# Second layer of a convolution and hard-swish kernel: P4's copies behind P2's C2, S2's chunks in another order, S4's negations behind the seed

## The chip, the cores and the metric

The kernel runs on one core of one Trainium2 chip. The metric is the device time of one execution in microseconds (us). Five engines of the core work side by side, each through its own instructions in order: TensorE (PE in the profile, its weight loads PEld), VectorE (DVE), ScalarE (ACT), GpSimd (POOL) and SyncE (SP). GpSimd and SyncE also issue transfers (DMAs). Semaphores order the engines among each other; they are put in by the framework from the order in which the program issues its instructions.

## The reference

```python
def _attn_ref(x, weight):                 # x (8, 4096, 192), weight (8, 7)
    w = np.exp(weight - np.max(weight, axis=-1, keepdims=True))
    w = w / (np.sum(w, axis=-1, keepdims=True) + 1e-09)
    x_pad = np.concatenate([np.zeros((B, K - 1, D)), x], axis=1)
    x_unf = x_pad[:, idx, :].reshape(B, S, K, H, group)
    return np.einsum('hk,bskhg->bshg', w, x_unf).reshape(B, S, D)

def _moe_ref(x, w_in, w_out):             # x (32768, 192), w_in (192, 2048), w_out (2048, 192)
    h = x @ w_in
    g = h * np.clip(h + 3.0, 0.0, 6.0) / 6.0
    return (g @ w_out).astype(np.float32)
```

A causal convolution of seven taps, one set of taps for each head, is followed by two matrix products with a hard-swish between them.

## The kernel before

The 32768 tokens are cut into 32 blocks of 1024. Block 0 is done in a plain way; blocks 1 to 31 each run `first_layer` and then `second_layer`. The first layer (matmuls of line 511) forms h from three parts of y (HIGH, LOW, MIX) and writes the gated g. The second layer (matmuls of line 653) forms g times w_out, and the change lies there.

**The fast product.** g is one tile of 8 chunks with four quarters each: A11, A21, A12, A22. w_out has B11, B12, B21, B22. The product is taken by a scheme of seven products in place of eight, with sums of the quarters as operands: S1 (kept in A21's place), S2 = S1 - A11 (kept in A11's place), S3 (a tile of its own, called `s` in the profile) and S4 = A12 - S2, which replaces S3 in its tile. Product 1 is A11 B11, 2 is A12 B21, 3 is S4 B22, 4 uses A22, 5 uses S1, 6 uses S2, 7 uses S3. Their results are called P1 to P7. Parts of products 1, 2, 4 and 5 are taken once more by the same scheme, at half size; those small products are written n.m here, so 2.7 is the seventh small product of product 2. Their operand sums lie in `shared` (of product 1), `sums2` (tile `z`, of 2), `sums4` (of 4) and `s5` (of 5, kept in A22's place).

**Accumulators.** PSUM is one tile of 8 banks, 128 rows by 512 columns each. In the second layer the banks are called x_, b, y_, c, a, f and h. Rows go by quadrants of 32: `first`, `second`, `third`, `fourth`; `lo` and `hi` are the halves of the columns, `m` the first 96 rows. The chains of the small products lie in x_ and y_: chain 2 (of P4) in rows 64 to 95 and chain 3 (of P1, later P5) in rows 96 to 127, each with A and E in the two halves of x_, and B and C in those of y_. A2, E2, B2, C2 and D2, the places of P2's small products, lie in f and h. A chain is continued by copies of ScalarE: B starts from a copy of A, C from a copy of B.

**The schedule.** The order is written out by hand. Four streams of matmuls, one for each strip of 32 output rows (strips 0 to 3), are put on a clock of 80 units; a matmul with 512 columns costs 2 units and runs as two passes, one with 256 columns costs 1. All other work is put among them by `do(t, ...)`, and everything is issued in order of these times, with t counted from half a unit earlier:

```python
def do(t, fn, *args, **kw):
    streams[3].append((t - 0.5, lambda: fn(*args, **kw)))
...
events = sorted(((t, fn) for st in streams for t, fn in st), key=lambda x: x[0])
```

So a number in `do` is a place in the order, for ScalarE, VectorE, GpSimd and SyncE each, not a time.

**What the steps below speak of**, by line:

- `level_two` (lines 740 to 754): the small products of P4 (strip 2, units 0 to 36), P1 (strip 3, units 0 to 36) and P5 (strip 3, units 44 to 76), each followed by its copy. Copies of step 1 are line 743 (B from A, here called B3 for P5), 2 line 744, 6 line 745 (C from B), 5 line 746, 7 line 747, 3 line 748. P4 is gathered in `shared`, P1 in `z`.
- Lines 815 and 816: two copies of b's first quadrant into P4's third. They must come before the seed, which overwrites that quadrant.
- Line 819: C2 from B2, wanted by small product 2.7 on strip 0 at unit 36. Line 820: D2 from B2, wanted at unit 60. Line 822: a copy inside bank a, wanted by strip 3 at unit 40; line 824 another, wanted at unit 60.
- The fill: product 5's matmuls on strip 3 that write the fourth quadrant of bank b, at units 4, 36, 48 and 76 (lines 760 and 761). "The fill" below is that of units 36 to 40.
- Line 841: S2 by pairs of chunks 02, 13, 46, 57 (line 458 in the profile, `g<-g`). S1, which it reads, comes from transfers that add two neighbouring chunks at a time. Product 6 reads S2 from unit 44 on.
- `fold` (lines 709 to 711): two sums of VectorE on P1 or P4; the second reads the chain's B in bank y_.
- Lines 844, 845 and 849: the small sums of S1 (line 603 in the profile, `g<-g`), wanted by P5's small products from unit 52 on.
- Line 847, the seed: P1 is copied to the first 96 rows of bank b (line 650, `psum<-z`), on which product 6 adds from unit 44.
- Line 851, the negations: S4 is made by ScalarE (line 572, `s<-g`: S3's tile becomes minus S2) and by a transfer that GpSimd issues (line 569) and that adds A12. Product 3 reads it from unit 64, in chunk order 0, 2, 1, 3, 4, 6, 5, 7.
- `between` (line 1125): split_high (ScalarE, line 476, at 48.4) and split_low (VectorE, line 1080, at 57) make parts of the next block's y.
- Lines 852 and 853: P7 is copied from bank c, and U3 is the sum of bank b and P7 (VectorE, line 458), to be read before product 3 adds to b at unit 64.

Of the kernel before, what the change touches and what calls it, by code (L numbers as in the profile page):

```python
# [25 lines left out]
def kernel(  # L26
# [8 lines left out]
    nc = tc.nc  # L35
# [10 lines left out]
    D2 = P // 2  # L46
# [41 lines left out]
    for base, dma in ((0, nc.scalar), (D2, nc.sync)):  # L88
        dma.dma_start(
            out=w_sb[base : base + D2],  # L90
            in_=weight.unsqueeze(1).to_broadcast([H, GJ, KC]),
# [126 lines left out]
    for n in range(AHEAD):  # L218
# [8 lines left out]
        out=e_sb[:], in0=w_sb[:], in1=mx[:].to_broadcast([P, KC]), op=ALU.subtract  # L227
# [47 lines left out]
    S2, S1, S4 = A11, A21, A12  # L275
# [5 lines left out]
    def take():  # L281
        return free_banks.pop(0)
# [163 lines left out]
    def rows(q):  # L446
        return slice(q * QS, (q + 1) * QS)
# [9 lines left out]
    def add(out, x, y, op=ALU.add):  # L457
        nc.vector.tensor_tensor(out=out, in0=x, in1=y, op=op)  # L458
# [126 lines left out]
    chunk_pairs = [slice(n, n + 3, 2) for n in (0, 1, 4, 5)]  # L585
# [35 lines left out]
    def second_layer(i, between):  # L621
        last = i + 1 == NB
        ours = [free_slots.pop(0) for _ in range(3)]
        x_, b, y_, c, a, _ = (psum[:, 2 * n + k] for n in ours for k in range(2))
# [3 lines left out]
        s5 = A22  # L628
        copy = nc.scalar.copy
        m = slice(0, DH)  # L630
        lo, hi = halves
        both = nc.sync, nc.scalar
        first, second, third, fourth = (rows(q) for q in range(4))
# [5 lines left out]
        A2, E2, C2, B2, D2 = f[first, lo], f[second, hi], h[first, lo], h[second, hi], h[third, hi]  # L639
# [3 lines left out]
        clock = [0] * 4  # L643
# [5 lines left out]
        def do(t, fn, *args, **kw):  # L649
            streams[3].append((t - 0.5, lambda: fn(*args, **kw)))  # L650
# [23 lines left out]
        def small(n, m_, out, start=False, j=3):  # L674

            x, w = prod[n]
            sums, ws = {
                1: (shared, w_s[:, 0]), 5: (s5, w_s[:, 1]), 2: (sums2, w_s[:, 2]),
                4: (sums4[0], w_s[:, 3]),
            }[n]  # L680
            x11, x12, x21, x22 = four_parts(x)
            z1, z2, z3, z4 = four_parts(sums)
            b11, t3, b21, b22 = quarters(w)
            t1, t2, t4 = (ws[:, k] for k in range(3))
            xm, wm = {
                1: (x11, b11), 2: (x12, b21), 3: (z4, b22), 4: (x22, t4),
                5: (z1, t1), 6: (z2, t2), 7: (z3, t3),
            }[m_]
            for u in range(NP // 2):
                put(j, 1, lambda u=u: matmul(  # L690
                    j, out, wm[:, u], xm[:, u], start and u == 0
                ))
# [45 lines left out]
        p4 = Fourth()  # L738

        def level_two(n, p, order, j=3):  # L740
            A, E, B, C = chains[j]
            steps = {
                1: lambda: copy(out=B, in_=A),
                2: lambda: copy(out=p()[first, lo], in_=A),  # L744
                6: lambda: copy(out=C, in_=B),
                5: lambda: copy(out=p()[second, lo], in_=E),
                7: lambda: copy(out=p()[second, hi], in_=C),
                3: lambda: copy(out=p()[first, hi], in_=C),
            }
            to = {1: A, 2: A, 6: B, 5: E, 7: C, 3: B, 4: C}  # L750
            for k in order:
                small(n, k, to[k], k in (1, 5), j)
                if k != 4:
                    do(clock[j] + (8.1 if k == 2 and n != 5 else 0.02 if n == 4 else 0), steps[k])

        rest = 6, 2, 7, 5, 4, 3
        chunks, first_fill = list(every), [True]
# [31 lines left out]
        p3(1)  # L789

        level_two(4, lambda: p4, (1,), 2)
        plain(2, c, 7, 2, every[:4], True)
        level_two(4, lambda: p4, rest, 2)
        plain(2, c, 7, 2, every[4:])
        plain(2, b, 6, 2, every)
        small(2, 3, D2, False, 2)
        p3(2)

        level_two(1, lambda: p1, (1,))
        fill_half(0, 2) if last else fill(2)  # L800
        plain(3, a, 2, 2, every[2:5] if last else every[2:4], True)
# [11 lines left out]
        assert clock == [80] * 4  # L813

        for t in halves:
            do(30 if t == hi else 29, copy, out=p4[third, t], in_=b[first, t])
        do(25.5, copy, out=p1[third], in_=b[second])
        do(20, copy, out=B2, in_=A2)
        do(31.9, copy, out=C2, in_=B2)
        do(45, copy, out=D2, in_=B2)  # L820
        do(12, copy, out=a[second], in_=a[fourth])
        do(34, copy, out=a[fourth], in_=a[second])
        do(40, lambda: copy(out=p2(second, hi), in_=C2))
# [13 lines left out]
        do(7, small_sums, sums2, A12, (3, 2), nc.vector)  # L837
        do(7, small_sums, sums4[0], A22, (4,), nc.vector)
        do(7, small_sums, sums2, A12, (1,), nc.vector)
        for r, when in zip(chunk_pairs, (28.5, 32.5, 28.6, 36.1)):  # L840
            do(when, lambda r=r: add(S2[:, r], S1[:, r], A11[:, r], ALU.subtract))
        do(32, tiles)
        do(36.03, fold_with, p1)
# [2 lines left out]
        do(36.05, fold_with, p4, 2)  # L846
        do(40 if last else 38.7, copy, out=b[m], in_=p1)
        do(21, last_sum, sums2, A12)
        do(36.3, small_sums, s5, S1, (1, 4), nc.vector)
        for r, t in zip(chunk_pairs, (30.5, 36.3, 42.1, 44.2)):  # L850
            do(t, negative, r)
        do(56.5, lambda: copy(out=late["p7"], in_=c[m]))
        do(60.2, lambda: add(late["u3"], b[m], late["p7"]))
# [83 lines left out]
    with tc.manual_schedule():  # L937
# [4 lines left out]
            out=c_sb[:], in0=e_sb[:], in1=sm[:].to_broadcast([P, KC]), op=ALU.mult  # L942
# [14 lines left out]
        b = take()  # L957
        for _ in range(3):

            nc.tensor.matmul(  # L960
                out=psum[:, b], lhsT=zeros[:, 0:P], rhs=zeros[:], start=True, stop=True
# [58 lines left out]
        n = 3  # L1020
        for slot, (c, group) in enumerate(parts):
            first = slot < len(early)
# [92 lines left out]
        for i in range(1, NB):  # L1115
            jobs = {n: [tap] for n, tap in zip((-1, 1, 3, 5, 7), taps)}
            jobs[-1] = left + jobs.get(-1, [])
            first_layer(i, jobs)
            def begin_conv():
                x_tiles[i + 2] = load_x(i + 2)  # L1120
                conv[:] = conv_jobs(i + 2)

            between, conv = [], []
            if i + 1 < NB:
                between += [(48.4, split_high), (57, split_low), (70, split_mix)]
                between += [
                    (t, lambda n=n: swap_parts(nc.gpsimd, (n,)))
                    for n, t in ((HIGH, 69), (LOW, 69), (MIX, 71))
                ]
            if i + 2 < NB:  # L1130
                between += [(1, begin_conv), (61.5, lambda: conv[0]()), (62, lambda: conv[1]())]
            left = second_layer(i, between)
            taps = conv[2:]
# [33 lines left out]
```

## Time and profile before

| | |
|---|---|
| median of 3 runs | 2220.82 us (2220.43 to 2220.97) |
| the profiled execution | 2220.51 us |
| its span in the profile | 2218.7 us |
| TensorE busy | 2201.0 us, 99% |
| VectorE busy | 1985.3 us, 89% |
| ScalarE busy | 1741.4 us, 78% |
| GpSimd busy | 1182.7 us, 53% |
| granted TensorE clock | 0.999 |

A block from the second on takes 68.07 us: about 35 in the second layer (80 units, of 0.43 us each) and 33 in the first. How to read the profile: times are us from the start of the span; a row names the engine, the line of the kernel, the operation, and the tiles as written and read. Matmuls are pipelined and their ends are modelled, so a stop of TensorE is read best from where its matmuls start. Idle time before an instruction is put down to the releaser that came last. The block shown below starts its second layer at 1017.95.

### The profile page before, as it was taken

To read this page: it belongs to the slowest core of one execution; us is meant where nothing else is said; L and a number is where in the kernel's file an instruction comes from. 1 tells how busy PE (TensorE), PEld (TensorE's weight loads), DVE (VectorE), ACT (ScalarE), POOL (GpSimd) and SP (SyncE) were. 2 spreads that over 40 slices of the span, in tenths; PEclk is the share of its full clock that TensorE was granted. 3 is DMA by queue.
4 is the path that set the end of the run, shared out by engine and by line. 5 is a ranking of instruction groups with operands and counts; after the bars stand their busy time and mean duration, and the time that the engine had idled before them with its cause. 6 is when DMAs were issued, how large, how long until landed. Compare 5 with 4: busy or idle time off the path is not lost.

```text
span 2218.7 us, 55332 instructions
## 1 busy us (share of the span) xinstructions
PE 2201.0 (99%) x22984; PEld 1481.5 (67%) x22984; DVE 1985.3 (89%) x1983; ACT 1741.4 (78%) x2391; POOL 1182.7 (53%) x1033
## 2 busy tenths in 40 slices
PE   9999999999999999999999999999999999999998
PEld 5467666667766676666677666766667666667765
DVE  8898998889898989988999988989898998889877
ACT  7488787787877878877878778787788787787876
POOL 2456544565544666445655446564456544565544
PEclk9999999999999999999999999999999999999999
DMA  6277778777778777787777888777877778777777
GB/s 157 60 137 146 141 145 151 141 145 141 145 138 159 136 141 143 146 156 133 146 142 145 144 151 143 141 139 144 160 131 145 139 147 153 138 146 140 132 141 117
DMA packets 353308, 313.20 MB, mean 141 GB/s; under 512 B 212480, under 2 KB 265216, under 8 KB 353056
## 3 DMA queue, kind: packets, MB, share of 16 engines
q0 software_dynamic: 114976, 234.46, 58.9%
q1 hardware_dynamic: 236840, 74.93, 16.7%
q8 instruction: 180, 2.95, 0.5%
q14 instruction: 72, 0.59, 0.1%
q10 hardware_dynamic: 1240, 0.27, 0.1%
HBM read 31.72 MB, written 25.17 MB: 26 GB/s over the span
## 4 chain that ended last, share of the span: by engine, by line
PE 93%; ACT 4%; issue 1%; DVE 0%; DMA 0%; SPq 0%; DVEq 0%; ACTq 0%
PE psum L511 46%; PE psum L653 44%; PE psum L296 2%; PE psum L341 2%; ACT s L572 1%; ACT shared L650 1%; ACT z L744 1%; ACT shared L744 1%; ACT psum L650 1%; DMA x<-in_x_dram 0%; DVE shared L458 0%; DVE g L603 0%; SPq L100 0%; DVE shared L464 0%; DVE g L458 0%
## 5 line engine op out<-in xcount | busy, mean ns | idle before, releaser
L653 PE MATMUL psum<-g,w_out 128*32 128x512 f32 (+1 forms) x5968 | 825.7, 503 | 0.0
L306 DVE SCALAR_TENSOR_TENSOR g<-g,psum 128x1024 f32<-128x1024 f32 (+1 forms) x528 | 618.8, 1185 | 107.3 <-ACT g L302 106.9
L653 PE MATMUL psum<-s,w_out 128*32 128x512 f32 (+1 forms) x3024 | 713.7, 586 | 0.0
L302 ACT ACTIVATE g<-psum,half 128x1024 f32<-128x1024 f32 (+1 forms) x528 | 565.4, 1088 | 5.7 <-PE psum L511 4.9
L511 PE MATMUL psum<-y_own,w_in 64*128 64x512 f32 x4464 | 523.3, 389 | 0.0
L511 PE MATMUL psum<-y_other,w_in 64*128 64x512 f32 x4464 | 516.0, 386 | 0.0
L523 ACT ACTIVATE psum<-psum 128x1024 f32<-128x1024 f32 x465 | 468.7, 1008 | 48.7 <-PE psum L511 46.6
L653 PEld LDWEIGHTS psum<-g,w_out 128*32 128x32 f32 x5968 | 338.5, 110 | 245.5 <-issue 111.4
L511 PEld LDWEIGHTS psum<-y_own,w_in 64*128 64x128 f32 x4464 | 413.5, 184 | 117.7 <-issue 26.0
L511 PEld LDWEIGHTS psum<-y_other,w_in 64*128 64x128 f32 x4464 | 418.1, 184 | 87.8
L603 POOL TENSOR_TENSOR shared<-g,shared 128x256 f32<-128x256 f32 x248 | 357.6, 1442 | 88.4 <-DVE g L306 57.0
L1057 DVE SCALAR_TENSOR_TENSOR y<-x,c_sb,y 128x1536 f32<-128x1536 f32 x186 | 335.2, 1802 | 1.5 <-ACT y L1055 1.3
L653 PE MATMUL psum<-g,w_s 128*32 128x256 f32 x1488 | 283.3, 379 | 0.3 <-DVE g L603 0.3
L569 POOL DMA_DIRECT2D s<-g x124 | 148.4, 1197 | 214.1 <-PE psum L653 124.2
L653 PE MATMUL psum<-z,w_out 128*32 128x256 f32 x992 | 235.1, 380 | 9.0 <-ACT psum L650 9.0
L569 POOL DMA_DIRECT2D g<-g x124 | 181.8, 1530 | 103.9 <-DVE s L414 103.9
L653 PE MATMUL psum<-z,w_s 128*32 128x256 f32 x992 | 227.5, 379 | 0.0
L653 PEld LDWEIGHTS psum<-s,w_out 128*32 128x32 f32 x3024 | 192.8, 110 | 51.2 <-issue 14.0
L266 POOL DMA_DIRECT2D y_other<-y_own x90 | 48.1, 534 | 280.2 <-issue 280.2
L458 DVE TENSOR_TENSOR g<-g 128x1024 f32<-128x1024 f32 x124 | 149.0, 1222 | 43.6 <-PE psum L653 30.9
L603 POOL TENSOR_TENSOR shared<-g 128x256 f32<-128x256 f32 x124 | 91.9, 741 | 170.3 <-DVE g L306 170.3
L650 ACT COPY psum<-psum 32x512 f32<-32x512 f32 x186 | 82.9, 446 | 116.4 <-PE psum L653 113.3
(115 smaller groups left out, 2955.9 us busy)
## 6 DMA issues: line engine op xcount, KB each, us to landing
y_other<-y_own POOLq DMA_DIRECT2D x180, 384.0 KB, 7.8
g<-g POOLq DMA_DIRECT2D x124, 512.0 KB, 6.1
s<-g POOLq DMA_DIRECT2D x124, 512.0 KB, 6.4
z<-g POOLq DMA_DIRECT2D x62, 512.0 KB, 7.5
out_dram<-shared SPq DMA_DIRECT2D x378, 64.0 KB, 4.2
x<-in_x_dram SPq DMA_DIRECT2D x53, 388.5 KB, 5.7
z<-g SPq DMA_DIRECT2D x31, 512.0 KB, 3.3
stage<-in_moe_w_in_dram SPq DMA_DIRECT2D x16, 192.0 KB, 4.4
```

The source lines that it names most:

```text
L266: dma.dma_start(out=to[D2:P], in_=part[0:D2])
L296: nc.tensor.matmul(out=psum[:, b], lhsT=w[r], rhs=src, start=start, stop=stop, skip_group_check=onto,)
L302: nc.scalar.activation(r6, h, ACT.Relu, bias=half[:], scale=1.0 / 6.0)
L306: nc.vector.scalar_tensor_tensor(out=g_, in0=g_, scalar=1.0, in1=h, op0=ALU.min, op1=ALU.mult)
L458: nc.vector.tensor_tensor(out=out, in0=x, in1=y, op=op)
L511: nc.tensor.matmul(out=psum[:, 2 * slots[n] + k], lhsT=r32(w_in_parts[part][r, c, s]), rhs=r32(y_other[0][r, part, s] if group else y_own[ ...
L523: nc.scalar.mul(both(n), both(n), 4097.0)
L569: nc.gpsimd.dma_start(out=out, in_=x, accum_op=ALU.add)
L603: engine.tensor_tensor(out=o, in0=p, in1=q, op=op)
L650: streams[3].append((t - 0.5, lambda: fn(*args, **kw)))
L653: nc.tensor.matmul(out=out, lhsT=w, rhs=x, start=start, stop=True, tile_position=(0, j * QS), skip_group_check=True,)
L1057: jobs.append(lambda k=k: nc.vector.scalar_tensor_tensor(out=y[:], in0=x[:, :, k : k + N], scalar=c_sb[:, k : k + 1], in1=y[:], op0=ALU.mu ...
```

## The change

Only places in the order change; no instruction is added or removed. P4's step 2 copy moves from 28.1 to 39.3, the two copies of line 816 from 29 and 30 to 35 and 35.1, D2's copy from 45 to 39.6. S2 was taken by chunks 02, 46, 13, 57 and is taken by 02, 13, 46, 57, the last of them now behind the small sums 3 and 2 of S1. The second and fourth negations move from 36.3 to 39.7 and from 44.2 to 48.3.

```diff
@@ -751,7 +751,8 @@
             for k in order:
                 small(n, k, to[k], k in (1, 5), j)
                 if k != 4:
-                    do(clock[j] + (8.1 if k == 2 and n != 5 else 0.02 if n == 4 else 0), steps[k])
+                    late_by = {(1, 2): 8.1, (4, 2): 19.3}.get((n, k), 0.02 if n == 4 else 0)
+                    do(clock[j] + late_by, steps[k])
 
         rest = 6, 2, 7, 5, 4, 3
         chunks, first_fill = list(every), [True]
@@ -813,11 +814,11 @@
         assert clock == [80] * 4
 
         for t in halves:
-            do(30 if t == hi else 29, copy, out=p4[third, t], in_=b[first, t])
+            do(35.1 if t == hi else 35, copy, out=p4[third, t], in_=b[first, t])
         do(25.5, copy, out=p1[third], in_=b[second])
         do(20, copy, out=B2, in_=A2)
         do(31.9, copy, out=C2, in_=B2)
-        do(45, copy, out=D2, in_=B2)
+        do(39.6, copy, out=D2, in_=B2)
         do(12, copy, out=a[second], in_=a[fourth])
         do(34, copy, out=a[fourth], in_=a[second])
         do(40, lambda: copy(out=p2(second, hi), in_=C2))
@@ -837,7 +838,7 @@
         do(7, small_sums, sums2, A12, (3, 2), nc.vector)
         do(7, small_sums, sums4[0], A22, (4,), nc.vector)
         do(7, small_sums, sums2, A12, (1,), nc.vector)
-        for r, when in zip(chunk_pairs, (28.5, 32.5, 28.6, 36.1)):
+        for r, when in zip(chunk_pairs, (28.5, 32.5, 32.6, 36.3)):
             do(when, lambda r=r: add(S2[:, r], S1[:, r], A11[:, r], ALU.subtract))
         do(32, tiles)
         do(36.03, fold_with, p1)
@@ -846,8 +847,8 @@
         do(36.05, fold_with, p4, 2)
         do(40 if last else 38.7, copy, out=b[m], in_=p1)
         do(21, last_sum, sums2, A12)
-        do(36.3, small_sums, s5, S1, (1, 4), nc.vector)
-        for r, t in zip(chunk_pairs, (30.5, 36.3, 42.1, 44.2)):
+        do(36.4, small_sums, s5, S1, (1, 4), nc.vector)
+        for r, t in zip(chunk_pairs, (30.5, 39.7, 42.1, 48.3)):
             do(t, negative, r)
         do(56.5, lambda: copy(out=late["p7"], in_=c[m]))
         do(60.2, lambda: add(late["u3"], b[m], late["p7"]))
```

On ScalarE the order from unit 28 to 48.4 was: P1's and P4's step 5, P4's step 2, P1's step 2, the two copies of line 816, negation 02, C2, a, P1's and P4's step 3, negation 13, seed, a copy of P2, negation 46, two copies of P2, negation 57, D2, B3, a, split_high. It becomes: P1's and P4's step 5, P1's step 2, negation 02, C2, a, the two copies of line 816, P1's and P4's step 3, seed, P4's step 2, D2, negation 13, a copy of P2, negation 46, two copies of P2, B3, a, negation 57, split_high.

## The prediction

> **What bounds the kernel now.** I read the busy shares first, then the groups with idle time on TensorE, then who waited for whom, then one block of the second layer in order of time on each engine. The page (engine, busy time, share, count; then one group with its idle time and releaser):
>
> ```profile
> PE 2201.0 (99%) x22984; PEld 1481.5 (67%) x22984; DVE 1985.3 (89%) x1983; ACT 1741.4 (78%) x2391; POOL 1182.7 (53%) x1033
> L653 PE MATMUL psum<-z,w_out 128*32 128x256 f32 x992 | 235.1, 380 | 9.0 <-ACT psum L650 9.0
> ```
>
> TensorE sets the time, so only what stops or releases it counts. Its one regular stop is 9.0 us in all, for a copy of line 650. The waits (engine, line, releaser: total, times, longest):
>
> ```profile
> PE psum L653 <- ACT psum L650: 9.0, 31, 0.3
> DVE z L458 <- ACT shared L748: 16.9, 22, 1.4
> ```
>
> 31 times is once for each second layer (the last block has a somewhat different schedule and is counted like the others); these repeat with the same offsets to 0.01 us in nearly all of them, so one block stands for all. The stop in the block that begins at 1017.95, in TensorE's order of time (start, us, instruction):
>
> ```profile
> 1033.30 0.38 PE L653 MATMUL psum<-shared,w_out 128*32 128x256 f32 x1
> 1033.97 0.40 PE L653 MATMUL psum<-z,w_out 128*32 128x256 f32 x1 [0.29 <-ACT psum L650]
> 1033.98 0.62 PE L653 MATMUL psum<-s,w_out 128*32 128x512 f32 x2
> 1033.99 0.62 PE L653 MATMUL psum<-g,w_out 128*32 128x512 f32 x1
> ...
> 1035.30 0.59 PE L653 MATMUL psum<-g,w_out 128*32 128x512 f32 x1
> ```
>
> This is unit 36 of 80. The z pass is product 2.7 and needs C2; the g pass is strip 3's fill of bank b, whose last pass starts at 1035.30. A 256-column pass follows the one before on its strip by 0.216 us, so strip 3 was due at 1033.52: the true loss is 1033.99 - 1033.52 = 0.47 us a block, 31 x 0.47 = 14.6 us in all, more than the 9.0 listed, since modelled ends cover part of it. Now ScalarE in the same block:
>
> ```profile
> 1031.08 0.36 ACT L744 COPY shared<-psum 32x256 f32<-32x256 f32 x1
> 1031.46 0.37 ACT L744 COPY z<-psum 32x256 f32<-32x256 f32 x1
> 1031.85 0.63 ACT L650 COPY shared<-psum 32x256 f32<-32x256 f32 x2
> 1032.50 1.06 ACT L572 ACTIVATE s<-g 128x1024 f32<-128x1024 f32 x1
> 1033.58 0.91 ACT L650 COPY psum<-psum 32x256 f32<-32x256 f32 x2
> ...
> 1034.91 0.36 ACT L748 COPY shared<-psum 32x256 f32<-32x256 f32 x1
> ...
> 1036.26 0.59 ACT L650 COPY psum<-z 96x512 f32<-96x512 f32 x1
> ...
> 1040.42 0.34 ACT L743 COPY psum<-psum 32x256 f32<-32x256 f32 x1
> ...
> 1041.27 1.48 ACT L476 ACTIVATE y_own<-y 128x1536 fp32r<-128x1536 f32 x1
> ```
>
> From 1030.3 to 1042.75 ScalarE has no gap. C2 is the first 0.34 us of the 1033.58 row; ahead of it stand P4's copies (1031.08 and the two of 1031.85) and a negation. The seed of P1 is at 1036.26. After split_high (1041.27) VectorE follows, and TensorE after it:
>
> ```profile
> 1035.31 0.43 DVE L458 TENSOR_TENSOR z<-psum,z 32x256 f32<-32x256 f32 x1 [1.36 <-ACT shared L748]
> 1042.79 1.76 DVE L1080 TENSOR_TENSOR y_own<-y,y_own 128x1536 fp32r<-128x1536 f32 x1 [0.36 <-ACT y_own L476]
> 1044.62 0.69 DVE L458 TENSOR_TENSOR shared<-psum,shared 96x512 f32<-96x512 f32 x1
> ...
> 1046.03 0.60 PE L653 MATMUL psum<-s,w_out 128*32 128x512 f32 x3
> 1046.07 0.59 PE L653 MATMUL psum<-g,w_s 128*32 128x256 f32 x2
> ```
>
> The 1044.62 sum (U3, ends 1045.31) reads bank b before product 3 adds to it at 1046.03 (unit 64): 0.72 us of slack. The 1035.31 row decides most: P1's second fold reads rows 96-127 of bank y_, yet starts 0.03 us after a ScalarE copy that reads rows 64-95 of it (1034.91 + 0.36). So the program orders accesses of a whole bank, other rows and mere reads included. The fill shows the same in the other direction: its last pass carries a semaphore update, at 1035.93, and only the seed, which writes rows 0-95 of b, can want it, the fill writing rows 96-127.
>
> **C2 and the fill.** P4's first copy goes (0.38) and two more move behind C2 and the copy after it (0.65 to the next row). P1's copy then starts at 1031.08, the negation at 1031.47, C2 at 1032.55, ending 1032.89. Product 2.7 was due at 1033.44: that wait is gone. But P4's two copies read b's first rows and are now issued just ahead of the fill, which writes b. They come behind C2 (0.36) and the 0.55 copy: 1033.49 and, 0.27 later, 1033.76, ending 1034.12. With the 0.05 us from a copy's end to TensorE's restart (1033.92 to 1033.97) the fill starts at 1034.17 instead of 1033.99: **+0.18**. Before, the same two copies ended at 1032.48 and the dependency cost nothing. No row shows TensorE waiting for another strip's reader; the bounds are no wait (strip 3 at 1033.52, -0.47) and +0.18, or +0.28 if the two copies don't overlap. I take +0.18, because both rows above show whole banks.
>
> By the Trainium skill (PSUM — Partial Sum Buffer, "PSUM bank collisions raise a hardware error") two engines in different 32-partition quadrants of one bank do not collide, so guarding by quadrant is enough and the fill would not wait. The 1.36 us on VectorE disagrees for what this program does; by the rule the first term would be -0.47.
>
> **The seed and ScalarE's queue.** The fill's update moves by the same 0.18, from 1035.93 to 1036.11, so the seed starts about 1036.13. Before, ScalarE filled the time up to it with a negation of 1.05; that now stands behind it. P4's last copy before the seed ends at 1034.90, so ScalarE idles 1.2 us. (Did the fill not wait, the seed would still stand until the fold, 1034.90 + 0.03 + 0.43, or the fill's update, 1035.46.) The idle time does not come back: the set of ScalarE instructions ahead of split_high is the same. From the seed: seed 0.61, P4's copy 0.38, D2 0.36, negation 0.97 to 1.08, P2's copy 0.39, negation 0.97, two copies 0.75, B3 0.37, copy of a 0.58, negation 0.97 to 1.08: 6.35 to 6.57, all by start-to-start distances of the same kinds. Split_high starts at 1042.48 to 1042.70, 1.2 to 1.4 late. On the way, the seed itself (ready 1036.8, wanted at 1037.44 + 0.18) is in time, and so is B3: it starts 4.46 behind the seed, ends at 1040.93, and its reader, 1040.89 before, is due at 1041.07. C3 behind split_high is at its limit, 0 to 0.06.
>
> **Unit 64.** U3's sum ends 4.03 us behind split_high's start (1.48 + 0.03 + 1.83 + 0.69): 1046.51 to 1046.73, and TensorE restarts 0.05 later, about 1046.66. Strip 3, the last of the four, stood at 1046.07 and would start some 0.02 behind the restart: 0.50 to 0.72 later than before, **0.6 as the middle**. This contains the 0.18; the rest is a second stop of about 0.4. The block ends as much later, as TensorE runs from there without a gap.
>
> **VectorE's order.** S2's 13 must wait for product 1's last use of chunk 3 (update at 1031.14), then 46, whose own wait (a transfer landing at 1031.06) is over: 1031.17 and 1032.31, ending 1033.53, as before (1033.50). Cost nothing, the cover being the fold's wait to 1034.9. In two of the 31 blocks that transfer lands late and the block is 0.24 and 0.45 longer; 13 in front takes out 1.14 of VectorE's lateness there: -0.7 in all. S5's sums go ahead by 1.14; their first user, at unit 52, is in time either way (1040.20 against 1040.81, when B3 frees it). S2's 57 ends at 1039.8 and its negation starts at 1041.5: hidden.
>
> **Moved transfers.** Each negation issues a POOL transfer, about 0.3 later and 1.2 long. The four move 2 MB at about 180 GB/s (windows of 2 us from 1036 to 1046 show 173 to 194), 2.85 us each, and the last lands 8.2 us after its issue. The three late ones are issued at 1038.8, 1040.3 and 1042.9, so the last lands by 1051.1 at the worst; chunk 5, wanted at 1051.18 before, is wanted at 1051.8. Hidden, by 0.7. POOL has nothing else until 1050.3. The stores on SP's queue follow U3 by 1.2; nothing on TensorE waits for them. The next first layer wants VectorE's gate at 1060.7 and had it at 1059.5; VectorE is 0.5 to 0.7 late against TensorE: covered.
>
> **The sum.** 31 x 0.6 - 0.7 = +18 on the profiled execution's 2220.5 (span 2218.7 and 1.8 around it); the median of the runs is 0.3 above that. **2238.5**, with its own range 31 x (0.35 to 0.8): 2231 to 2246.
>
> **Rivals.**
> - *The fill does not wait and the seed need not either* (guards by quadrant): the seed starts at 1034.9, U3 ends at 1045.4, before strip 3 comes at 1045.6, and all 0.47 are gained: 2220.8 - 14.6 - 0.7 = 2205.5. For it: the listed stop is really removed. Against: the two rows above. Chance 0.08. This is the faster side; it decides from the point where the fill starts at 1033.5. The rule of the Trainium skill named above (PSUM — Partial Sum Buffer) would lead here.
> - *The fill does not wait but the seed does*: seed 1035.48, U3 at 1046.0, stop of 0.4 at unit 64 eats the 0.47: about 2219.5. Chance 0.06.
> - *Only the first stop*: ScalarE makes up 0.4 behind the seed by overlaps as between the two copies (0.27 for 0.36), or VectorE does: 31 x 0.18 = 5.6, 2226. Chance 0.14. For it: some pairs overlap; against: the same set took 6.36 before.
> - *A third stop*: the last S3 piece lands 1 us later, as four transfers and the stores then share the queues: another 0.4, 31 x 0.4 = 12.4, 2251. Chance 0.09.
> - Forecast 0.63.
>
> No change means within 0.2% (4.4 us), about what a measurement can tell here. Faster is the first rival and some of the second, 0.10; same is the rest of the second and a little of the third, 0.07; slower 0.83. The range 2224 to 2250 takes in the forecast, the third rival and half of the fourth, and leaves out 0.18.
>
> **What would show it.** Right: TensorE's idle at unit 36 stays, now at a w_out pass on g and released by line 650; a new one at the first pass on s of unit 64, released by VectorE line 458; ScalarE waits about 1.2 us ahead of the seed; the period of a block goes from 68.07 to 68.7. Wrong: the fill starting at 1033.5 in this block's clock, or U3's sum still ending by 1045.4.

## The result and the profile after

The changed kernel takes 2226.94 us (median of 9 runs, 2226.65 to 2227.42); the kernel before, run beside it, 2220.82 us (9 runs). The ratio is 1.0028, 95% interval [1.0017, 1.0038]: slower by about 6 us. The profiled execution has a span of 2224.9 us against 2218.7.

The added 6.2 us of span lie in the second layers. Measured from a second layer's first matmul to its last, 28 of the 31 became longer by 0.25 to 0.27 us. The two in which a late transfer had cost time changed by less than 0.01 and by -0.21, and the last became shorter by 0.77: 6.3 in all. The first layers between them are the same to 0.01 us.

The same views of the profile after, first who waited for whom (engine, line, releaser: total, times, longest):

```profile
DVE z L458 <- ACT shared L748: 23.4, 30, 0.8
PEld psum L653 <- DVE shared L458: 14.3, 30, 0.5
PEld psum L653 <- ACT shared L650: 13.1, 31, 0.4
```

The stop released by C2 is gone, and two others stand in its place, seen on the weight loads, which run ahead of the matmuls. One is released by line 650 writing `shared`: these are P4's two copies out of bank b. The other is released by line 458 writing `shared`: this is U3's sum. TensorE in order of time, in the block that begins at 1020.96 (the views below are of that block):

```profile
1036.44 0.38 PE L653 MATMUL psum<-z,w_out 128*32 128x256 f32 x1
1036.44 0.66 PE L653 MATMUL psum<-s,w_out 128*32 128x512 f32 x2
1036.65 0.38 PE L653 MATMUL psum<-z,w_out 128*32 128x256 f32 x1
1036.88 0.66 PE L653 MATMUL psum<-s,w_out 128*32 128x512 f32 x2
1037.05 0.62 PE L653 MATMUL psum<-g,w_out 128*32 128x512 f32 x1
...
1049.30 0.63 PE L653 MATMUL psum<-s,w_out 128*32 128x512 f32 x3
1049.32 0.40 PE L653 MATMUL psum<-g,w_s 128*32 128x256 f32 x1
```

In microseconds from the block's own start, 2.7 begins on strip 0 at 15.48, when it is due. Strip 3's fill (the pass on g) begins at 16.10, and not at 15.57, when it is due; in the kernel before it began at 16.04. At unit 64 strip 3 begins at 28.36; before, at 28.12. ScalarE:

```profile
1034.09 0.37 ACT L744 COPY z<-psum 32x256 f32<-32x256 f32 x1
1034.36 1.05 ACT L572 ACTIVATE s<-g 128x1024 f32<-128x1024 f32 x1
1035.43 0.92 ACT L650 COPY psum<-psum 32x256 f32<-32x256 f32 x2
1036.37 0.62 ACT L650 COPY shared<-psum 32x256 f32<-32x256 f32 x2
...
1037.41 0.36 ACT L748 COPY shared<-psum 32x256 f32<-32x256 f32 x1
1038.99 0.59 ACT L650 COPY psum<-z 96x512 f32<-96x512 f32 x1 [1.22 <-PE psum L653]
...
1045.26 1.48 ACT L476 ACTIVATE y_own<-y 128x1536 fp32r<-128x1536 f32 x1
```

C2 ends at 1035.77, early enough. P4's two copies end at 1037.00, and the fill starts 0.05 later. Then ScalarE, which had no gap here before, stands idle for 1.22 us in front of the seed, released by TensorE: the seed waits for the fill's end. Split_high begins at 24.30 from the block's start, 0.98 later than before. VectorE behind it:

```profile
1037.81 0.43 DVE L458 TENSOR_TENSOR z<-psum,z 32x256 f32<-32x256 f32 x1 [0.83 <-ACT shared L748]
...
1046.77 1.76 DVE L1081 TENSOR_TENSOR y_own<-y,y_own 128x1536 fp32r<-128x1536 f32 x1 [1.82 <-ACT y_own L476]
1048.56 0.69 DVE L458 TENSOR_TENSOR shared<-psum,shared 96x512 f32<-96x512 f32 x1
```

Split_low now waits 1.82 us for split_high (0.36 before), U3's sum ends at 1049.24, and TensorE goes on 0.06 later, at 1049.30. P1's fold still starts 0.03 us after a copy out of other rows of its bank.

### The profile page after: what moved, and what is told of

The parts are those of the page before. It is cut to its first block, busy times and chain, and to the rows that moved or that the text cites. A ratio compares the mean times of both kernels' runs of the same rounds, so it can differ in the third digit from the quotient of the medians.

```text
span 2224.9 us, 55392 instructions
## 1 busy us (share of the span) xinstructions
PE 2216.5 (100%) x22984; PEld 1516.6 (68%) x22984; DVE 1985.6 (89%) x1983; ACT 1738.1 (78%) x2391; POOL 1182.2 (53%) x1033
## 4 chain that ended last, share of the span: by engine, by line
PE 99%; DVE 0%; ACT 0%; DMA 0%; SPq 0%; issue 0%; DVEq 0%; ACTq 0%
PE psum L653 49%; PE psum L511 46%; PE psum L296 2%; PE psum L341 2%; DMA x<-in_x_dram 0%; DVE shared L458 0%; DVE shared L464 0%; SPq L100 0%; SPq L133 0%; DVE top L175 0%; PE psum L953 0%; DVE y L255 0%; SPq L89 0%; ACT y L967 0%; ACT scale L186 0%
## 5 line engine op out<-in xcount | busy, mean ns | idle before, releaser
L653 PEld LDWEIGHTS psum<-g,w_out 128*32 128x32 f32 x5968 | 370.8, 110 | 254.5 <-issue 91.6
L653 PEld LDWEIGHTS psum<-s,w_out 128*32 128x32 f32 x3024 | 198.4, 110 | 77.3 <-issue 16.2
L653 PEld LDWEIGHTS psum<-g,w_s 128*32 128x32 f32 x1488 | 135.3, 110 | 52.7
```

Of the source, the lines that this page charges most:

```text
L653: nc.tensor.matmul(out=out, lhsT=w, rhs=x, start=start, stop=True, tile_position=(0, j * QS), skip_group_check=True,)
```

## The experiments

Times from here on are from the block's own start, unless a fence shows the span's. Each ratio is to the kernel before, run on the same chip, with its 95% interval. The theory was that of the prediction: the fill waits for the copies, the seed for the fill, ScalarE idles, and U3 is late. Rival A held that the copies' place costs nothing and the negation behind the seed everything; rival B that the sums' new order or late transfers cost it.

**e1: the copies back.**

```diff
 for t in halves:
-    do(35.1 if t == hi else 35, copy, out=p4[third, t], in_=b[first, t])
+    do(30 if t == hi else 29, copy, out=p4[third, t], in_=b[first, t])
```

> The changed kernel with P4's two copies of bank b back at 29 and 30, all else as changed. Theory (the fill on strip 3 waits for these copies because it writes the same bank; the seed waits for the fill, ScalarE idles, and U3 is late at unit 64): C2 ends some 0.8 us later than in the changed kernel and just misses strip 0 (a stop of 0.1 to 0.15 at unit 36, released by C2), the fill starts about 15.66 after the block's start in place of 16.10, the seed 17.6 in place of 18.04, U3's sum ends at 27.9 in place of 28.29, with a stop of about 0.2 left at unit 64: 2212 to 2216. Rival A (the copies' place costs nothing, the negation behind the seed alone costs the time): 2225 to 2228. Rival B (S2's and S5's new order or late transfers cost it): 2225 to 2228.

2214.12 us, 0.997 [0.9959, 0.9982]. The fill starts at 15.66, the seed at 17.62, U3's sum ends at 27.86. TensorE's waits:

```profile
PEld psum L653 <- DVE shared L458: 14.6, 30, 0.5
PEld psum L653 <- ACT psum L650: 13.4, 32, 1.2
```

The wait for the copies is gone, that for U3 stays, and a short one for C2 is back. A and B fall: each forecast no gain from this edit.

**e2: negation 13 back.**

```diff
-for r, t in zip(chunk_pairs, (30.5, 39.7, 42.1, 48.3)):
+for r, t in zip(chunk_pairs, (30.5, 36.3, 42.1, 48.3)):
```

> The changed kernel with negation 13 back at 36.3, ahead of the seed; the copies stay behind C2. Theory: the fill still waits for the copies (strip 3 at 16.10) and the seed for the fill (18.04), but ScalarE does the negation while it waits, split_high comes 1.1 us earlier and U3's sum ends near 27.2, so the stop at unit 64 goes: 2220 to 2223. Rival A (only the negation's place costs time, the fill would have been free): 2205 to 2212. Rival B: 2225 to 2228.

2220.51 us, 0.9999 [0.999, 1.0008]. The fill is at 16.10 as in the changed kernel, the seed at 18.03, U3's sum ends at 27.37. Now the other wait remains:

```profile
PEld psum L653 <- ACT shared L650: 13.1, 31, 0.4
...
1036.41 0.59 ACT L650 COPY psum<-z 96x512 f32<-96x512 f32 x1 [0.26 <-PE psum L653]
```

The negation runs while ScalarE waits for the fill; of the idle 1.22 only 0.26 is left (the second line, from the order of time). e1 and e2 take away one stop each and leave the other as it was, so there are two causes.

**e3: both back.** The edits of e1 and e2 together.

> Both of these: copies back at 29 and 30, negation 13 back at 36.3. Theory: only a stop of 0.1 at unit 36 for C2 is left, none at unit 64: 0.38 us a block below the kernel before, 2206 to 2210. Rivals A and B: A gives 2205 to 2212 as well, B 2225 to 2228.

2207.93 us, 0.9943 [0.9931, 0.9955]. A second layer is 34.21 long, 0.38 less than before. What is left is the stop for C2, which with the copies ahead of it lets 2.7 start 0.16 after it is due.

**e6: the copies early.** Bank b's first quadrant is final at unit 16. The two places in `shared` hold operand sums that are read up to units 16 and 24.

```diff
-    do(35.1 if t == hi else 35, copy, out=p4[third, t], in_=b[first, t])
+    do(26 if t == hi else 18, copy, out=p4[third, t], in_=b[first, t])
...
-for r, t in zip(chunk_pairs, (30.5, 39.7, 42.1, 48.3)):
+for r, t in zip(chunk_pairs, (30.5, 36.3, 42.1, 48.3)):
```

> The changed kernel with P4's two copies at 18 and 26, where ScalarE has idle time and the places that they write in the tile of P4 are no longer read, and negation 13 back at 36.3. Theory: C2 and the fill are both in time at unit 36 and U3 at unit 64, no stop is left in the second layer, and a block is 0.47 us shorter than in the kernel before: 2204 to 2207. Under theory B it stays at 2225.

2203.77 us, 0.9924 [0.9911, 0.9936]: the best version, 17 us below the kernel before and 0.2 below the range expected. Every second layer but the last is 34.09 long, 0.50 less than before. TensorE's busy share on the page:

```profile
PE 2193.5 (100%) x22984; PEld 1561.7 (71%) x22984; DVE 1985.9 (90%) x1983; ACT 1738.0 (79%) x2391; POOL 1182.2 (54%) x1033
```

In the list of its waits, line 653 waits for another engine only once, for 0.4 us in the last block.

**e5: the copies late, nothing else.** To the kernel before, only 35 and 35.1 for the two copies.

> The kernel before with only the two copies of bank b moved to 35 and 35.1; P4's first copy stays ahead of C2, the negation ahead of the seed. Theory: C2 ends near 15.2 and strip 0 runs on, but the copies end near 16.4 and the fill starts at 16.48 in place of 16.04: 0.44 us a block, no stop at unit 64: 2232 to 2236, slower than the whole change. Rival A (the place of the copies costs nothing): the stop at unit 36 is gone, 2205 to 2210.

2232.89 us, 1.0054 [1.0041, 1.0066]: twice the loss of the whole change. TensorE in one block, in order of time:

```profile
1038.85 0.38 PE L653 MATMUL psum<-z,w_out 128*32 128x256 f32 x1
1038.86 0.66 PE L653 MATMUL psum<-s,w_out 128*32 128x512 f32 x2
...
1039.84 0.62 PE L653 MATMUL psum<-g,w_out 128*32 128x512 f32 x1
```

Strips 0 to 2 begin unit 36 in time, at 15.49, and strip 3's fill only at 16.47, 0.43 later than before; its wait for line 650 writing `shared` grows to 24.9 us in all. With P4's first copy still ahead, the two copies end 0.38 later than in the changed kernel (16.42 and 16.04), and the fill starts 0.05 after their end in both.

**e7: the copies behind the fill.** The changed kernel with 38.6 and 38.65 for the copies, and negation 13 at 36.3.

> The changed kernel with the copies moved further back, to 38.6 and 38.65, behind the fill's last matmul in the order of issue, and negation 13 at 36.3. Theory (an order between the fill and the readers of its bank): now the copies wait for the fill and not the fill for them: fill at 15.57, copies from 17.5, seed at 18.15, no stop at unit 64: 2203 to 2207, like the early copies. Rival C (the fill is late because ScalarE's queue up to there is too long, whatever it holds): the fill stays near 16.0 and the time at 2220 or above.

2211.03 us, 0.9956 [0.9943, 0.9968]. The fill starts at 15.57 as in e6, so rival C, which had it stay near 16.0, falls. (The queue ahead of the fill is also shorter here, by the two copies. That the fill waits for these copies and not for a long queue is told by the releaser in the lists above and by the 0.05 us between their end and its start in e5 and in the changed kernel.) The copies start at 17.52, behind the fill:

```profile
1029.85 0.59 PE L653 MATMUL psum<-g,w_out 128*32 128x512 f32 x1
...
1031.80 0.62 ACT L650 COPY shared<-psum 32x256 f32<-32x256 f32 x2
1032.45 0.59 ACT L650 COPY psum<-z 96x512 f32<-96x512 f32 x1
1033.06 0.37 ACT L744 COPY shared<-psum 32x256 f32<-32x256 f32 x1
```

The fill's update comes at 17.51, but the negation ahead of the copies ends only at 17.49, so this run alone does not show that the copies wait. That a later access of ScalarE to bank b waits for the fill is shown by the seed, idle for 1.22 in the changed kernel. So whichever comes first in the order of issue holds up the other, though they touch different rows of the bank.

The time was missed by 4 us. The seed ends at 18.76, 0.18 before unit 44 is due; product 6 starts there as in e6 (18.93 and 18.99), but strip 3's first pass comes at 19.20 in place of 19.00, and the second layer is 0.23 longer than in e6. The trace shows why, and it is the same order once more. That pass is small product 5.1, which writes rows 96 to 127 of bank x_. P4's step 2 copy (the last line above), which stands behind the late seed, reads rows 64 to 95 of x_ until 19.15. The weight load of 5.1 starts at 19.20, released by that copy; in e6 the copy ends at 18.40 and the load does not wait. The expectation had left this second bank out.

**e8: early copies alone.** To the kernel before, only 18 and 26 for the two copies.

> The kernel before with only the two copies moved forward to 18 and 26. Theory: C2 ends near 15.2, before 2.7 is due at 15.48; nothing else was late, so the whole 0.47 us a block are gained and the rest of the change adds at most the 0.7 us of the two late blocks: 2203.5 to 2206. If D2, P4's first copy or the S2 and S5 orders carry some of the gain, it is over 2207.

2207.27 us, 0.9938 [0.9925, 0.995]: above the range expected, and 0.3 us over the point at which other parts were to carry some of the gain. In its profile 22 of 31 second layers are 34.09 long; the other nine are longer, the last block and eight more, these by 0.04 to 0.91. The cause is in VectorE's order of time in one of them:

```profile
959.79 2.36 DVE L458 TENSOR_TENSOR g<-g 128x1024 f32<-128x1024 f32 x2 [2.56 <-DMA g<-g]
```

S2's 46 waits for a transfer that lands late, and 13, P1's folds and the seed wait behind it: the seed comes at 18.68 in this block, and at 17.5 to 17.7 in those of 34.09.

**e4: S2's order alone.** To the kernel before, the diff's lines for S2 and for the small sums 1 and 4.

> The kernel before with only S2's order (02, 13, 46, 57 with 57 behind the small sums 3 and 2 of S1). Theory: the two blocks in which a late transfer held up the seed lose their extra 0.24 and 0.45 us, all others stay as they were: 2219.5 to 2220.5, within the measurement of no change. Rival B (this order or its later negation costs the time): 2225 to 2228.

2254.16 us, 1.0149 [1.0134, 1.0165]: a plain miss of the expectation. The regular second layers are 1.18 us longer each, and only the last is shorter, by 1.26. ScalarE in order of time, and the sum of the waits:

```profile
1055.43 1.06 ACT L572 ACTIVATE s<-g 128x1024 f32<-128x1024 f32 x1 [1.26 <-DVE g L458]
...
1056.88 0.34 ACT L743 COPY psum<-psum 32x256 f32<-32x256 f32 x1
...
PEld psum L653 <- ACT psum L743: 31.7, 30, 1.1
```

The order made S2's 57 later; negation 57, still at its old place, waits 1.26 us for it, and B3 (line 743) stands behind the negation. TensorE stops at unit 52: strip 3's first pass of it starts at 24.10, and at 22.94 before.

**e10: e4 with negation 57 at 48.3.**

> e4 (S2's order alone) with negation 57 moved from 44.2 to 48.3, behind B3. Theory (e4 lost its 33 us because negation 57 stood in ScalarE's queue waiting for S2's 57, now made later, with B3 behind it): the loss goes, the stop at unit 36 for C2 stays as in the kernel before: 2219 to 2221. If the order of the S2 and S5 sums itself costs the time, it stays near 2254.

2218.51 us, 0.999 [0.9981, 0.9999]. The loss of e4 is gone, and the time lies 0.5 us below the range expected. The regular second layers are as long as in the kernel before (34.58 to 34.59); the two with a late transfer are 0.25 and 0.46 shorter and the last 1.27. The order of the sums costs nothing once the negation has moved with it.

**e9: early copies and S2's 13 ahead of 46.** e8, and 32.6 in place of 28.6 for chunks 46; 57, the small sums and the negations stay.

> The kernel before with the two copies moved forward to 18 and 26, and S2's chunks 13 moved ahead of 46; 57, the small sums and the negations stay. Theory (what e8 lacked against e6 is the transfer that S2's 46 waits for: it stands in front of the seed whenever it lands late): 2203 to 2205, as e6, with no block above 34.1. If the other moves of the change carry the 3.5 us: 2206 to 2208, as e8.

2204.21 us, 0.9926 [0.9913, 0.9938]. Every second layer but the last is 34.09 long. Three numbers of the kernel before are enough for nearly all of e6's gain. What e6 changes besides (P4's first copy, D2, S2's 57 with the small sums, negation 57) is worth the 0.4 us between the two, which lie in the last second layer: 35.24 here, 34.87 in e6.

## Why the prediction failed

**Direction and places: right.** It forecast slower, by a fill that waits for P4's copies, a seed that waits for the fill, an idle ScalarE and a new stop at unit 64 for U3. The trace after shows all four, and e1, e2 and e5 show that each stop goes or grows with its cause.

**"C2 and the fill": the first term was mis-sized.** It said +0.18; measured +0.06 (16.04 to 16.10). The negation started 0.27 behind the copy ahead of it, and not 0.39, so C2 and the copies ended 0.13 earlier. The dependency itself was as forecast: a stop of 0.47 on strip 3 was exchanged for one of 0.53 (15.57 to 16.10).

The Trainium skill (PSUM — Partial Sum Buffer, "PSUM bank collisions raise a hardware error") says that different quadrants of one bank may be used at once. By it the first term would have been -0.47. The fill's wait for copies out of other rows of its bank (e5, and the changed kernel) disagrees for this program, whose semaphores keep order by whole banks; no run here shows whether the chip itself would have allowed it.

**"The seed and ScalarE's queue": the wait right, the lateness too long.** Idle 1.2 was forecast, 1.22 measured. The seed came at 18.03 and not 18.18, which follows from the fill. From the seed to split_high 6.35 to 6.57 was summed and 6.27 measured: the steps seed to P4's copy (0.53 for 0.61) and D2 to negation (0.27 for 0.36) overlapped, and the last negation took the short distance (0.96).

So "the idle time does not come back" was wrong by 0.23. The same 21 ScalarE instructions, from 12.36 to split_high, took 10.96 before; after, they took 11.94, of which 1.22 was idle, so the work itself took 10.72. In the new order six pairs of neighbours overlap, in the old one four. Split_high was 0.98 late and not 1.2 to 1.4.

**"Unit 64": the step that failed.** "0.50 to 0.72 later than before, 0.6 as the middle" measured 0.24 at unit 64 and 0.25 to 0.27 at the end of the block. The term is a difference: U3's lateness, forecast as 1.2 to 1.4, less 0.72 of slack. The lateness was 0.94 (27.35 to 28.29): split_high's 0.98, less 0.04 on VectorE. An error of a third of a microsecond in a sum of some dozen distances became more than half of the difference, and 31 blocks multiplied it: 31 x 0.6 - 0.7 = 18, where 28 regular blocks gave 7.3, the two with a late transfer -0.2 and the last -0.77. The last block had been counted like the others; e10, where it is 1.27 shorter, puts its gain down to the sums' order with negation 57's move. (By the same terms the range's upper end, 31 x 0.8 - 0.7, is 2245 and not 2246.)

**The rival "Only the first stop" gave 2226**, close to the result, but this was luck and not what happened: the first stop cost 0.06 and not 0.18, and the second was there. The range 2224 to 2250 takes the result in through this rival alone. e2, which has the first stop alone, takes 2220.5.

**"VectorE's order": right for the whole change** (the two late blocks came out 0.25 and 0.47 better than the others), wrong as "cost nothing" by itself: e4 shows that it needs negation 57's move, which the prediction priced only as hidden. And the 13 ahead of 46 is worth 3 us once TensorE is not late any more (e8 to e9), not only 0.7: the kernel before hid most late transfers behind the stop at unit 36 (S2's 46 at 14.63 left one of its second layers at 34.59; at 14.62 in e8 it cost 0.24).

**"Moved transfers": right.** No weight load waits for an S3 piece in the trace after.

## What to carry to other kernels

When work is moved out of the way of a late operand, ask what else the moved instruction touches: here it read the accumulator bank that the next matmul writes, so the wait changed its name and stayed. Look first for a place earlier in the order, in an idle stretch of the engine: that gained 14 to 17 us, where the place just ahead of the fill lost 6 (12 by itself) and the place behind the fill gained 10. And when a term is lateness less slack, the error of the whole chain stands against the small difference; its range should be as wide as that.

## What was not expected of the hardware

- ScalarE starts some instructions up to 0.09 us before the one ahead has ended (0.27 from start to start for a copy of 0.36) and others 0.02 after (0.39 for the same copy). Which pair overlaps was not settled.
- In e7 the weight loads of product 6 on strips 0 to 2 were held by the seed until 18.81, where in e6 the first began at 18.56, and their matmuls began at 18.93 to 18.99 in both: a load of 0.11 us that ended 0.02 before its matmul was due cost nothing here.
